# A gated linear-attention block and a PReLU network on one core: weight conversion reordered and split, gate products by scans, VectorE's order written out

## The chip, the cores and the metric

The kernel runs on one core of a Trainium2 chip. The metric is the device time of one execution in microseconds; three runs of the kernel before gave 783.32 us in the median (782.89 to 785.24). The core's engines are named as the profile names them: PE is TensorE (PEld its weight loads), DVE is VectorE, ACT is ScalarE, POOL is GpSimd, and SP is SyncE, which here only issues DMAs.

## What is computed

Two blocks follow each other. The first is an attention with a decaying state, for 4 batches of 8 heads, 768 positions and head dimension 48; the second is a network with one hidden layer of 2048 units on the 3072 rows (width 384) that the first one gives.

```python
f = 1.0 / (1.0 + np.exp(-f_logit))
for t in range(S):
    state = f[:, :, t, :, None] * state + np.einsum('bhd,bhe->bhde', k[:, :, t], v[:, :, t])
    y[:, :, t] = np.einsum('bhd,bhde->bhe', q[:, :, t], state)
x = y.transpose(0, 2, 1, 3).reshape(B * S, H * D)
h = x @ w_in                                            # 384 x 2048
g = np.maximum(h, 0.0) + alpha * np.minimum(h, 0.0)
out = g @ w_out                                         # 2048 x 384
```

All inputs are 32-bit floats but the two weight matrices, which arrive as 64-bit floats. The kernel turns them into 32-bit floats on the chip: each 64-bit value is read as two 32-bit words, and exponent, mantissa and sign are rebuilt with integer and float operations.

## The kernel before, in words

The work is cut into 12 chunks: 2 batches (U) by 128 positions (C), in the order of `steps`. The main loop runs over 13 steps; step n does the attention of chunk n and the network of chunk n-1, so that TensorE has network matmuls to do while VectorE works on the attention.

**Preparation of a chunk** (before the first `yield` of `attention`). The gate f goes through a sigmoid on ScalarE (L163). VectorE forms products of neighbouring gates: `kr` and `fq` within groups of four positions (L174 to L178), `qd`, the queries times one to three gates (L182, 3 operations), `us`, the queries times products of gates over further groups (L187 and six at L196), and `k4`, the keys times gates (L191). `pre` and `suf`, the running gate products from the left and from the right over the eight groups of a block of 32, are made on GpSimd by doubling (L203 to L212: a memset, a copy and 14 multiplications). Seven VectorE operations then make `q3`, `ks`, `kh` and `f64` from them (L222 to L232).

**Stages of a chunk** (five, with a `yield` behind each). For each of the two batches: TensorE makes `raw` (L246) and `qu` (L262), and VectorE copies the wanted parts into `ad` with predicated copies (L253, 4 of them; L267, 7 of them): these are stages 1 and 2. Stage 3: `off` (L280) and the transpose `pk` (L288), which ScalarE copies to `ksn` (L291). Stage 4: `pd` (L301) and the new states on VectorE (L311 to L315). Stage 5: ScalarE spreads `ad` and `off` into `A` (L323, L327), TensorE makes `py` (L336, L347), ScalarE copies it to `y` (L352), and ten DMAs issued by SP carry it into `xT` (L358), the network's input. `raw`, `qu`, `off`, `pk`, `pd` and `py` take turns in two PSUM buffers (tag `pair`).

**The network of a chunk.** In eight pieces of 256 hidden units: six matmuls to a PSUM bank `ph` (L371; the profile counts each as two), ScalarE makes `neg`, the part below zero (L376), and VectorE adds it back scaled, two operations to `g` (L379). Then for each batch 16 matmuls to `po` (L386), a copy on ScalarE (L389) and a DMA out. `ph` and `po` take turns in four PSUM banks.

**The weights** are converted by `load_weights` in 24 pieces of 512 columns, 12 for each matrix: a DMA issued by ScalarE (L129) and seven VectorE operations (L134 to L143). The pieces of `w_in` are called behind the stages of step 0 and those of `w_out` behind the stages of step 1, each matrix in the order in which it lies in memory: for `w_in` the whole first third of the input rows, then the second, then the third.

**The order of the work.** `tc.manual_schedule` takes TensorE's order as the program writes it: within a step two pieces of the network follow stage 1, two follow stage 2, then one, two and one, and all of `po` comes at the end of the step. All other engines run in the order that a scheduler finds. Each engine runs its instructions strictly one after another; an instruction that waits holds up those behind it, the DMA issues on SP's and ScalarE's queues too.

## Time and profile before

| what | value |
|---|---|
| median of the runs | 783.32 us |
| the profiled execution's own time | 781.1 us |
| its span, first to last instruction | 779.2 us |
| PE busy | 658.2 us (84%) |
| PEld busy | 485.5 us (62%) |
| DVE busy | 435.6 us (56%) |
| ACT busy | 159.1 us (20%) |
| POOL busy | 70.6 us (9%) |
| mean granted TensorE clock | 0.936 |

All rows of the trace are those of the profiled execution; 1.9 us of its time lie outside the span. In the views, a row of a group gives its line, engine and operation, what it writes and reads, its shapes and count, then after the bar the busy time in all and the mean of one in ns, and then the idle time of the engine just before these instructions with what ended it. In a timeline the first two numbers are the start and the length in us, and a bracket gives the idle time before.

### The profile page before, as it was taken

How to read it: one execution, taken by the hardware profiler on the slowest of the kernel's cores; microseconds unless marked ns; L12 is line 12 of the kernel's file. 1: busy time of each engine (PE TensorE's matmuls, PEld its weight loads, DVE VectorE, ACT ScalarE, POOL GpSimd, SP SyncE). 2: the span in 40 equal slices, each digit the busy share in tenths (PEclk: the TensorE clock that was granted, in tenths of full speed). 3: DMA queues.
4: the chain of work that ended last, by engine and by line, in shares of the span. 5: the costliest groups of instructions: out<-in, count | busy, mean ns of one | idle time of the engine just before them, and what ended most of it. 6: DMA issues, size and time to landing. Idle time of an engine off the chain costs nothing.

```text
span 779.2 us, 17567 instructions
## 1 busy us (share of the span) xinstructions
PE 658.2 (84%) x7712; PEld 485.5 (62%) x7712; DVE 435.6 (56%) x920; ACT 159.1 (20%) x289; POOL 70.6 (9%) x228
## 2 busy tenths in 40 slices
PE   0350186468999999899999999999999999999998
PEld 0350175124876777777867857768778678587684
DVE  5798997892861842933916808618439157052030
ACT  2030023000330411410411403204104114041110
POOL 8212002000020020020020100200200200000000
PEclk9995589557999999999999999999999999999999
DMA  4224432440220210211212202202101110000000
GB/s 177 83 84 122 159 105 76 135 145 26 69 67 21 84 42 22 83 41 28 80 48 66 56 24 70 65 22 83 41 23 55 51 40 8 24 13 22 21 0 21
DMA packets 31468, 46.79 MB, mean 60 GB/s; under 512 B 3744, under 2 KB 19104, under 8 KB 31392
## 3 DMA queue, kind: packets, MB, share of 16 engines
q1 hardware_dynamic: 27648, 33.04, 14.2%
q10 hardware_dynamic: 3744, 12.63, 5.1%
q8 instruction: 61, 1.00, 0.5%
q14 instruction: 15, 0.12, 0.1%
HBM read 36.22 MB, written 4.72 MB: 53 GB/s over the span
## 4 chain that ended last, share of the span: by engine, by line
PE 67%; DVE 21%; DMA 5%; POOL 3%; ACT 1%; issue 1%; SPq 1%; ACTq 0%; DVEq 0%; POOLq 0%
PE po L386 31%; PE ph L371 24%; PE py L336 3%; DVE qd L182 3%; PE py L347 3%; DVE g L379 2%; DVE ad L267 2%; PE raw L246 2%; DMA qd<-in_qT 2%; DVE ad L253 2%; PE pd L301 2%; PE pk L288 2%; PE qu L262 1%; DMA w_in_raw<-in_w_in 1%; DMA w_out_raw<-in_w_out 1%; DVE k L191 1%
## 5 line engine op out<-in xcount | busy, mean ns | idle before, releaser
L371 PE MATMUL ph<-xT,w_in_sb 128*128 128x256 f32 x1152 | 269.2, 390 | 37.5 <-DVE w_in_sb L143 37.5
L386 PE MATMUL po<-w_out_sb,g 128*128 128x384 f32 x768 | 264.5, 504 | 29.3 <-DVE w_out_sb L143 29.3
L371 PEld LDWEIGHTS ph<-xT,w_in_sb 128*128 128x128 f32 x1152 | 218.4, 194 | 73.0 <-DVE w_in_sb L143 39.2
L386 PEld LDWEIGHTS po<-w_out_sb,g 128*128 128x128 f32 x768 | 149.0, 196 | 140.5 <-DVE w_out_sb L143 32.9
L253 DVE COPY_PREDICATED ad<-mraw,raw 128x256 f32<-128x256 int32 x96 | 42.7, 444 | 174.6 <-PE raw L246 172.4
L379 DVE SCALAR_TENSOR_TENSOR g<-neg,om,ph 128x256 f32<-128x256 f32 x192 | 84.3, 475 | 72.5 <-ACT neg L376 72.2
L376 ACT ACTIVATE neg<-ph 128x512 f32<-128x512 f32 x96 | 57.3, 597 | 201.6 <-PE ph L371 131.8
L389 ACT COPY o<-po 128x384 f32<-128x384 f32 x24 | 11.5, 478 | 278.5 <-PE po L386 278.5
L267 DVE COPY_PREDICATED ad<-mquad,qu 128x224 f32<-128x224 int32 (+6 forms) x168 | 49.7, 296 | 5.2 <-DVE ad L253 0.5
L246 PE MATMUL raw<-qd,k 48*32 48x128 f32 x1536 | 29.4, 286 | 19.4 <-DVE qd L182 19.4
L196 DVE TENSOR_TENSOR us<-us,fq 128x768 f32<-128x768 f32 (+2 forms) x72 | 44.3, 615 | 0.0
L203 POOL MEMSET suf<- 128x256 f32 x12 | 3.7, 311 | 418.4 <-DVE ks L225 418.4
L246 PEld LDWEIGHTS raw<-qd,k 48*32 48x32 f32 x1536 | 22.8, 110 | 28.5 <-POOL pre L212 19.4
L262 PE MATMUL qu<-us,k 48*32 48x116 f32 x1536 | 27.3, 273 | 12.4 <-DVE us L196 6.9
L323 ACT COPY A<-ad 32x512 f32<-32x512 f32 x48 | 29.6, 617 | 20.1 <-DVE ad L267 19.7
L262 PEld LDWEIGHTS qu<-us,k 48*32 48x32 f32 x1536 | 22.5, 109 | 13.7 <-DVE us L196 7.3
L232 DVE TENSOR_TENSOR f<-pre 128x16 f32<-128x16 f32 x12 | 2.2, 184 | 47.8 <-POOL pre L212 47.7
L210 POOL TENSOR_TENSOR suf<-suf,pre 128x32 f32<-128x32 f32 (+2 forms) x84 | 28.8, 368 | 1.8
L182 DVE TENSOR_TENSOR qd<-qd,f 128x768 f32<-128x768 f32 (+2 forms) x36 | 27.5, 764 | 1.9 <-DMA qd<-in_qT 1.8
L336 PE MATMUL py<-A,v 128*64 128x128 f32 x384 | 24.9, 285 | 2.5 <-DVE us L196 2.5
L288 PE MATMUL pk<-ident,ks 128*128 128x128 f32 x96 | 13.9, 291 | 14.5 <-DVE ad L267 11.7
L336 PEld LDWEIGHTS py<-A,v 128*64 128x64 f32 x384 | 22.0, 143 | 6.3 <-issue 6.3
(60 smaller groups left out, 429.8 us busy)
## 6 DMA issues: line engine op xcount, KB each, us to landing
f<-in_fT SPq DMA_DIRECT2D x12, 512.0 KB, 3.7
k<-in_kT SPq DMA_DIRECT2D x12, 512.0 KB, 5.5
qd<-in_qT SPq DMA_DIRECT2D x12, 512.0 KB, 4.0
w_in_raw<-in_w_in ACTq DMA_DIRECT2D x12, 512.0 KB, 3.5
w_out_raw<-in_w_out ACTq DMA_DIRECT2D x12, 512.0 KB, 3.5
v<-in_v SPq DMA_DIRECT2D x12, 384.0 KB, 3.3
out<-o SPq DMA_DIRECT2D x24, 192.0 KB, 1.9
xT<-y SPq DMA_DIRECT2D x72, 48.0 KB, 2.0
```

The costliest lines, as they stand in the source:

```text
L182: nc.vector.tensor_tensor(quads(qdv[d])[:, :, d:4], quads(qdv[d - 1])[:, :, d:4], f[:, :, 1:5 - d], ALU.mult)
L196: nc.vector.tensor_tensor(us[:, :, UO[m]:UO[m] + 4 * n].rearrange("p g (i r) -> p g i r", r=4), us[:, :, skip:skip + 4 * n].rearrange("p g ...
L246: nc.tensor.matmul(raw[DB * j:DB * (j + 1), par, hp * C:(hp + 1) * C], lhsT=k[r_, g:g + DB], rhs=qd[r_, 0:4 * W].rearrange("p (d x) -> p d ...
L253: nc.vector.copy_predicated(adu, mraw[:, d].rearrange("p i r -> p (i r)").bitcast(I32).unsqueeze(1).broadcast_to((128, H, DB)), rv[:, :, d])
L262: nc.tensor.matmul(qu[DB * j:DB * (j + 1), par, hp * UW:(hp + 1) * UW], lhsT=k4[r_, g * DB:(g + 1) * DB], rhs=us[r_, g], start=True, stop= ...
L267: nc.vector.copy_predicated(ad[:, u, :, :, 4 * m:DB], mquad[:, lo:lo + n].bitcast(I32).unsqueeze(1).unsqueeze(1).broadcast_to((128, 2, HP, ...
L323: nc.scalar.copy(A[s_, :, :, s_], ad[s_].rearrange("p u r h t -> p u (r h) t"))
L336: nc.tensor.matmul(py[64 * par:64 * par + 64, u, hp * C:(hp + 1) * C], lhsT=vt[:, u, hd * D:hd * D + 64], rhs=A[:, u, par * HP + hp], star ...
L371: nc.tensor.matmul(ph[:, j * T:(j + 1) * T], lhsT=w_in_sb[:, kt, (f + j) * 128:(f + j + 1) * 128], rhs=xT[:, kt], start=(kt == 0), stop=(k ...
L376: nc.scalar.activation(neg, phv, AF.Relu, scale=-1.0)
L379: nc.vector.scalar_tensor_tensor(g[:, j], neg[:, j], om[:, f + j:f + j + 1], phv[:, j], ALU.mult, ALU.add)
L386: nc.tensor.matmul(po[:, 0:DM], lhsT=gs[f // 2][:, f % 2, u * C:(u + 1) * C], rhs=w_out_sb[:, f], start=(f == 0), stop=(f == NF - 1))
```

## The change

1. **Conversion.** Per piece five VectorE operations instead of seven, and one on ScalarE: the exponent field is masked out on VectorE, shifted to its new base on ScalarE (an activation with a scale and a bias, clamped at zero), and sign and mantissa are joined by shifts and ORs on whole integers, where the old code built a float mantissa by parts. Each piece has its own buffers (four for the raw words). The DMAs of the pieces are issued by SP instead of ScalarE.
2. **Order of the pieces.** `w_in` is converted in groups of three pieces, one of each third of the input rows, so that three pieces serve the first two `ph` of a network. `load_weights` is a generator whose pieces are called one by one between other work.
3. **Gate products.** `pre` and `suf` come from two scans on VectorE per chunk, of 289 elements each, in place of GpSimd's 16 operations. The factors lie in `fs` with a zero between blocks, and `ones` restarts the product there. GpSimd keeps one small memset per chunk.
4. **Order.** VectorE's order is now written out too. The preparation of a chunk is a sequence of seven pieces. A step is a string of calls: S is a stage of the chunk, P a piece of its own preparation, Q a piece of the next chunk's, n a piece of the network of the chunk before, w and v a piece of `w_in` and `w_out`. Steps 0 to 3 have strings of their own.
5. **Network.** The two `po` of a chunk are filled side by side, four f at a time in pieces of their own (12 pieces per network in all).
6. **Smaller edits.** Queries are loaded into a tile of their own and copied to `qd` by ScalarE (1024 elements); five of the ten `xT` DMAs are issued by ScalarE; `om` is made by ScalarE instead of VectorE; GpSimd's memsets of `qd` and `kr` at the start cover only what needs it; several tiles have one buffer less (`v`, `y`, `q3`, `ks`, `kh`: one; `neg`: two; `g`: eight).

```diff
-    nc.vector.tensor_scalar(om, om, -1.0, 1.0, ALU.mult, ALU.add)
+    nc.scalar.activation(om, om, AF.Identity, bias=1.0, scale=-1.0)
...
-        for n in range(0, flat.shape[1], WP):
-            raw = work.tile([128, WP, 2], I32, tag="y", name=f"{name}_raw{n}")
-            nc.scalar.dma_start(out=raw.rearrange("p n two -> p (n two)"),
-                                in_=src[:, n:n + WP].bitcast(I32))
+        ks = NK if dst is w_in_sb else 1
+        per = flat.shape[1] // ks
+        for n in [k * per + j for j in range(0, per, WP) for k in range(ks)]:
+            raw = work.tile([128, WP, 2], I32, tag="raw", name=f"{name}_raw{n}", bufs=4)
+            nc.sync.dma_start(out=raw.rearrange("p n two -> p (n two)"),
+                              in_=src[:, n:n + WP].bitcast(I32))
             lo, hi = raw[:, :, 0], raw[:, :, 1]
-            mi = work.tile([128, WP], I32, tag="neg", name=f"{name}_mi{n}", bufs=3)
-            nc.vector.tensor_scalar(mi, hi, 0xFFFFF, 0x100000, ALU.bitwise_and, ALU.bitwise_or)
-            m = mi.bitcast(F32)
-            nc.vector.scalar_tensor_tensor(m, lo.bitcast(U32), 2.0 ** -32, mi, ALU.mult, ALU.add)
-            e = work.tile([128, WP], I32, tag="neg", name=f"{name}_e{n}", bufs=3)
-            nc.vector.tensor_scalar(e, hi, 20, 0x7FF, ALU.logical_shift_right, ALU.bitwise_and)
-            nc.vector.tensor_scalar(e, e, 1023.0 - 127.0, 0.0, ALU.subtract, ALU.max)
-            nc.vector.tensor_scalar(e, e, 255.0, 2.0 ** 23, ALU.min, ALU.mult)
+            e = work.tile([128, WP], I32, tag="e", name=f"{name}_e{n}")
+            nc.vector.tensor_scalar(e, hi, 0x7FF00000, None, ALU.bitwise_and)
+            nc.scalar.activation(e, e, AF.Relu, bias=bias, scale=8.0)
+            m = work.tile([128, WP], U32, tag="m", name=f"{name}_m{n}")
+            nc.vector.tensor_scalar(m, hi.bitcast(U32), 11, 0x80000000, ALU.logical_shift_left, ALU.bitwise_or)
+            nc.vector.scalar_tensor_tensor(m, lo.bitcast(U32), 21, m, ALU.logical_shift_right, ALU.bitwise_or)
             nc.vector.scalar_tensor_tensor(e, hi, -0x80000000, e, ALU.bitwise_and, ALU.bitwise_or)
-            nc.vector.scalar_tensor_tensor(flat[:, n:n + WP], m, 2.0 ** -20, e.bitcast(F32), ALU.mult, ALU.mult)
+            nc.vector.scalar_tensor_tensor(flat[:, n:n + WP], m, 2.0 ** -31, e.bitcast(F32), ALU.mult, ALU.mult)
+            yield
...
-        h = 1
-        while h < NB:
-            for n in range(0, NB, 2 * h):
-                lo, up = slice(n, n + h), slice(n + h, n + 2 * h)
-                nc.gpsimd.tensor_tensor(suf[:, :, lo], suf[:, :, lo],
-                                        pin[:, :, n + 2 * h - 1:n + 2 * h].broadcast_to((128, G, h)), ALU.mult)
-                nc.gpsimd.tensor_tensor(pin[:, :, up], pin[:, :, up],
-                                        pin[:, :, n + h - 1:n + h].broadcast_to((128, G, h)), ALU.mult)
-            h *= 2
+        ps = work.tile([128, NS], F32, tag="ps", name=f"ps_{i}", bufs=1)
+        nc.vector.tensor_tensor_scan(ps, fs, ones, 0.0, ALU.mult, ALU.add)
+        ss = work.tile([128, NS], F32, tag="ss", name=f"ss_{i}", bufs=1)
+        nc.vector.tensor_tensor_scan(ss[:, ::-1], fs[:, ::-1], ones[:, ::-1], 0.0, ALU.mult, ALU.add)
...
-                nc.sync.dma_start(
+                (nc.sync if hd % 2 else nc.scalar).dma_start(
...
+    first = (
+        "P7 S w S w S w S w S w2",
+        "n w n w n w n w n w n w n2 P7 S v S v S v S v2 S v n2 v3 n v3 n",
...
+    usual = "S n Q n S n Q n S Q n S Q n Q n S Q2 n5"
```

What this moves shows at three places. First VectorE at the start of the first network, where `g_0_0` is made: the last conversion of `w_in` in the kernel before,

```order
L134 TENSOR_SCALAR w_in_mi_578<-w_in_raw_576 128x512
L143 SCALAR_TENSOR_TENSOR w_in_sb<-w_in_mi_567,w_in_e_570 128x512
L136 SCALAR_TENSOR_TENSOR w_in_mi_578<-w_in_raw_576,w_in_mi_578 128x512
L139 TENSOR_SCALAR w_in_e_581<-w_in_raw_576 128x512
L140 TENSOR_SCALAR w_in_e_581<-w_in_e_581 128x512
L379 SCALAR_TENSOR_TENSOR g_0_0_729<-neg_0_0_727,om,ph_0_0_720 128x256
```

and the same place now, where the seventh of twelve pieces stands behind the first `g`:

```order
L394 SCALAR_TENSOR_TENSOR g_0_0_520<-neg_0_0_518,om,ph_0_0_511 128x256 x2
L148 TENSOR_SCALAR w_in_e_525<-w_in_raw_523 128x512
L152 TENSOR_SCALAR w_in_m_528<-w_in_raw_523 128x512
L153 SCALAR_TENSOR_TENSOR w_in_m_528<-w_in_raw_523,w_in_m_528 128x512
L154 SCALAR_TENSOR_TENSOR w_in_e_525<-w_in_raw_523,w_in_e_525 128x512
L155 SCALAR_TENSOR_TENSOR w_in_sb<-w_in_m_528,w_in_e_525 128x512
L394 SCALAR_TENSOR_TENSOR g_0_0_542<-neg_0_0_540,om,ph_0_0_533 128x256 x2
L148 TENSOR_SCALAR w_in_e_547<-w_in_raw_545 128x512
```

Before, the first `g` stands in the last of the twelve pieces; now six pieces come ahead of it and one piece behind each of the first six `g`.

Second, VectorE in the middle of a usual step: the copies out of the second `qu` of a chunk into `ad`, before, with work for the next chunk (`k`, `qd`) between them,

```order
L379 SCALAR_TENSOR_TENSOR g_1_1_2356<-neg_1_1_2354,om,ph_1_1_2347 128x256 x2
L253 COPY_PREDICATED ad<-mraw,raw_0_2_2359 128x256 x4
L267 COPY_PREDICATED ad<-mquad,qu_0_2_2396 128x8x28
L191 TENSOR_TENSOR k_1_2_2682<-k_2_2667,kr 128x1024
L267 COPY_PREDICATED ad<-mquad,qu_0_2_2396 128x8x24
L182 TENSOR_TENSOR qd<-qd,f_2_2663 128x256x3
L267 COPY_PREDICATED ad<-mquad,qu_0_2_2396 128x8x20
L182 TENSOR_TENSOR qd<-qd,f_2_2663 128x256x2
```

and now:

```order
L394 SCALAR_TENSOR_TENSOR g_1_2_3243<-neg_1_2_3241,om,ph_1_2_3234 128x256 x2
L182 TENSOR_TENSOR kr<-f_3_3246 128x256
L183 TENSOR_TENSOR kr<-f_3_3246,kr 128x256
L186 TENSOR_TENSOR fs<-f_3_3246,kr 128x32x8
L394 SCALAR_TENSOR_TENSOR g_1_2_3266<-neg_1_2_3264,om,ph_1_2_3257 128x256 x2
L266 COPY_PREDICATED ad<-mraw,raw_0_3_3269 128x256 x4
L280 COPY_PREDICATED ad<-mquad,qu_0_3_3306 128x8x28
L280 COPY_PREDICATED ad<-mquad,qu_0_3_3306 128x8x24
L280 COPY_PREDICATED ad<-mquad,qu_0_3_3306 128x8x20
```

The three gate products of the next chunk now come ahead of these copies, and nothing comes between the copies; `qd` follows behind the next `g`.

Third, ScalarE at the end of the first chunk's attention, where `y` is copied. Before, DMA issues for weights follow the copy,

```order
L163 ACTIVATE f_1_1663<-f_1_1663 128x1024
L352 COPY y_0_442<-py_0_409 128x512 x2
L129 DMA w_in_raw_455<-in_w_in 128x1024
L129 DMA w_in_raw_466<-in_w_in 128x1024
L129 DMA w_in_raw_477<-in_w_in 128x1024
```

and now five issues for `xT` (two alike in the fifth row), and behind them the exponents of the fifth and sixth piece of `w_in`:

```order
L365 COPY y_0_477<-py_0_444 128x512 x2
L372 DMA xT_0_480<-y_0_477 48x2x128
L372 DMA xT_0_480<-y_0_477 32x2x128
L372 DMA xT_0_480<-y_0_477 16x2x128
L372 DMA xT_0_480<-y_0_477 48x2x128 x2
L149 ACTIVATE w_in_e_493<-w_in_e_493,bias 128x512
L149 ACTIVATE w_in_e_503<-w_in_e_503,bias 128x512
L391 ACTIVATE neg_0_0_518<-ph_0_0_511 128x512
```

The exponents of two conversions now queue behind DMA issues on ScalarE, and VectorE's conversion of those pieces waits for them.

126 lines of the change are left out of this document (68 added, 58 removed), and 2 rows, old and new, of the table first.

## The prediction

> **What bounds the kernel now.** I read the page's slices first, then the windows by stage, then who waited for whom, then the timelines of PE and DVE. The slices, 19.5 us each, show two kernels in one:
>
> ```profile
> PE   0350186468999999899999999999999999999998
> DVE  5798997892861842933916808618439157052030
> PEclk9995589557999999999999999999999999999999
> ```
>
> In the first ten slices DVE is full, PE is mostly idle, and PE's clock drops to half. Behind them PE is full. The windows put numbers on it; a row gives the window, its length, then the busy time of PE, PEld, DVE, ACT and POOL, and the granted clock:
>
> ```profile
> 0.00:194.80 194.80, 88.82 (x1072) 58.88 (x1072) 152.10 (x304) 26.06 (x43) 32.47 (x93) 0.75 0.35 111
> 194.80:359.50 164.70, 159.51 (x1945) 119.66 (x1944) 88.14 (x189) 39.33 (x72) 14.41 (x51) 0.99 0.18 52
> 359.50:681.90 322.40, 315.89 (x3897) 237.16 (x3902) 173.29 (x372) 76.08 (x141) 23.70 (x84) 1.00 0.16 47
> 681.90:734.50 52.60, 52.60 (x650) 39.82 (x650) 15.07 (x39) 11.38 (x22) 0.00 (x0) 1.00 0.06 17
> 734.50:779.20 44.70, 41.33 (x160) 30.02 (x158) 6.98 (x16) 6.21 (x11) 0.00 (x0) 1.00 0.04 14
> 413.20:466.90 53.70, 52.65 (x657) 39.55 (x661) 29.31 (x63) 13.13 (x24) 4.80 (x17) 1.00 0.19 53
> ```
>
> 194.8 us go by before step 2 starts: the start. Steps 2 to 4 take 164.7 us, steps 5 to 10 322.4 us (53.7 each, of which PE is busy 52.65, one of them in the last row), step 11 52.6 us, the last network 44.7 us. So a usual step has 1.05 us to give, and the start has some 130 us in which PE is not at work at full clock. The waits name the two places (us in total, times, longest):
>
> ```profile
> PE ph L371 <- DVE w_in_sb L143: 37.5, 3, 17.2
> PE po L386 <- DVE w_out_sb L143: 29.3, 12, 9.0
> PE pk L288 <- DVE ad L267: 11.7, 9, 2.4
> DVE f L232 <- POOL pre L212: 47.7, 10, 4.8
> ```
>
> PE's large waits are for converted weights. `pk` waits for the predicated copies nine times. The 47.7 us that DVE waits for POOL's products are cover: DVE has over 20 us of idle time in a usual step.
>
> **The change, part by part.** First the prices. A conversion now:
>
> ```profile
> 80.27 0.43 DVE L134 TENSOR_SCALAR w_in_mi<-w_in_raw 128x512 int32<-128x512 int32 x1
> 101.67 0.42 DVE L134 TENSOR_SCALAR w_in_mi<-w_in_raw 128x512 int32<-128x512 int32 x1
> L142 DVE SCALAR_TENSOR_TENSOR w_in_e<-w_in_raw,w_in_e 128x512 int32<-128x512 int32 x12 | 8.3, 690 | 0.3
> L376 ACT ACTIVATE neg<-ph 128x512 f32<-128x512 f32 x96 | 57.3, 597 | 201.6 <-PE ph L371 131.8 <-DVE w_in_sb L143 48.3 <-issue 19.3
> ```
>
> The two L134 are six pieces apart: 3.57 us a piece, where four short operations (0.43) and three long ones (0.69) add up to 3.79, so starts overlap by 6%. The new piece has two short and three long: 2.93 by durations, 2.8 as I take it; 24 of them save 24 x 0.77 = 18 us of DVE. The exponent goes over ScalarE: 0.6 us by `neg`, the same size; on integers it is not in the trace, and I bound it by half and double that. It runs beside the two DVE operations between (0.43 + 0.69 = 1.1 us), so it is free if ScalarE takes it at once, and costs what ScalarE is late if not. The Trainium skill ("ScalarE: Activation LUTs", What ACT_TABLE_LOAD costs) gives an activation with a bias from memory 280 ns plus 0.833 ns per element, here 0.71 us; by it the sum would be up to 24 x 0.1 = 2.4 us longer. No row here has such a bias.
>
> The preparation of a chunk on DVE:
>
> ```profile
> L174 DVE TENSOR_TENSOR kr<-f 128x256 f32<-128x256 f32 x12 | 7.6, 633 | 1.9 <-POOL kr L116 1.9
> L182 DVE TENSOR_TENSOR qd<-qd,f 128x768 f32<-128x768 f32 (+2 forms) x36 | 27.5, 764 | 1.9 <-DMA qd<-in_qT 1.8
> L187 DVE TENSOR_TENSOR us<-qd,f 128x1024 f32<-128x1024 f32 x12 | 24.1, 2011 | 0.0
> L191 DVE TENSOR_TENSOR k<-k,kr 128x1024 f32<-128x1024 f32 x12 | 14.6, 1216 | 0.0
> L196 DVE TENSOR_TENSOR us<-us,fq 128x768 f32<-128x768 f32 (+2 forms) x72 | 44.3, 615 | 0.0
> L222 DVE TENSOR_TENSOR q<-us,pre 128x512 f32<-128x512 f32 x24 | 16.3, 680 | 0.0
> ```
>
> Per chunk: three like L174 (1.9), `qd` 27.5/12 = 2.3, `us` 2.0 and 44.3/12 = 3.7, `k4` 1.2, and six like L222 with a tiny one (4.1): 15.2 us. Two scans come on top. No row shows one: 289 elements by L174 would be 0.7 us, by L222 0.4; as each element waits for the one before it could be double the slower, 1.4, and a gain is excluded because DVE had no such work. I take 0.5 each, near L222, whose operands lie side by side as the scan's do: 16.2 us per chunk. The Trainium skill ("DVE: opcode table, instruction layouts, handler registers and perf-mode slots", Datapath and trigger behaviour) has this scan run at half throughput; by it two preparations in the start would be 4 x 0.4 = 1.6 us longer; no row of this trace shows it. In usual steps DVE's idle time hides either. GpSimd's products cost nothing where they were, and going they gain nothing but the 3 us that `kh` waited once in the start.
>
> The copies of one batch into `ad`, and a pair of `g`:
>
> ```profile
> 360.73 1.89 DVE L253 COPY_PREDICATED ad<-mraw,raw 128x256 f32<-128x256 int32 x4 [18.62 <-PE raw L246]
> 362.72 2.29 DVE L267 COPY_PREDICATED ad<-mquad,qu 128x224 f32<-128x224 int32 x7
> 364.99 0.87 DVE L379 SCALAR_TENSOR_TENSOR g<-neg,om,ph 128x256 f32<-128x256 f32 x2
> ```
>
> 4.3 us for the eleven copies, 0.87 for the `g`. The start and the way out of the first chunk:
>
> ```profile
> 1.67 1.28 ACT L163 ACT_TABLE_LOAD   x1 [1.67 <-PEq L472]
> 4.52 1.06 ACT L163 ACTIVATE f<-f 128x1024 f32<-128x1024 f32 x1 [1.57 <-DMA f<-in_fT]
> 9.34 0.64 DVE L174 TENSOR_TENSOR kr<-f 128x256 f32<-128x256 f32 x1 [1.85 <-POOL kr L116]
> 41.50 1.97 PE L288 MATMUL pk<-ident,ks 128*128 128x128 f32 x8 [1.44 <-ACT A L327]
> 49.10 3.26 PE L336 MATMUL py<-A,v 128*64 128x128 f32 x32 [2.51 <-DVE us L196]
> 52.29 1.10 PE L347 MATMUL py<-q,state 48*48 48x64 f32 x32
> 53.93 0.59 ACT L352 COPY y<-py 128x512 f32<-128x512 f32 x1
> 54.54 6.94 SPq L358 DMA_DIRECT2D xT<-y  x10
> 62.96 1.22 PE L371 MATMUL ph<-xT,w_in_sb 128*128 128x256 f32 x2 [7.30 <-DVE w_in_sb L143]
> ```
>
> *Up to the first `ph`.* `om` on ScalarE brings a second table load of 1.28 us ahead of the sigmoid, which ends near 7.4 instead of 5.6; but DVE waited for GpSimd's memset of `kr` until 9.34, and that wait goes. DVE starts at 7.4, ends the preparation at 23.6, copies of batch 0 at 27.9, a weight piece at 30.7, copies of batch 1 at 35.0. Now PE has `pk` to `py`, which took 11.9 us (41.50 to 53.39) with a 2.5 us wait in it: 9.4, done at 44.4. On DVE weight pieces and the states lie beside it. `y` takes 1.1 us; the ten `xT` issues take 0.69 us each on one queue, so five on each of two 3.5 us; landing took 1.5 us (61.48 to 62.96). First `ph` at 50.5, with its weights there.
>
> *The first network and w_in.* The first `ph` runs at half clock. These two rows are the same twelve matmuls, at half clock in part and warm:
>
> ```profile
> 113.38 4.37 PE L371 MATMUL ph<-xT,w_in_sb 128*128 128x256 f32 x12
> 212.09 2.76 PE L371 MATMUL ph<-xT,w_in_sb 128*128 128x256 f32 x12
> 392.45 20.80 PE L386 MATMUL po<-w_out_sb,g 128*128 128x384 f32 x64
> ```
>
> With 4.8 us for it, `neg` and `g`, DVE stands at 56.9. From here DVE is the pace: six pieces and five `g`, 6 x 2.8 + 5 x 0.87 = 21.2, to 78.1. The last two `ph`, partly cold, 6.8, then `neg` and `g` 1.5: 86.4. PE's other six `ph` lie under the pieces.
>
> *Second chunk and w_out.* Preparation 16.2 to 102.6; twice 4.3 of copies, six pieces (16.8) and three state operations of at most 0.68: 27.4, to 130. Two exponents queue behind five `xT` issues on ScalarE (3.5 us); I add 3: 133. Six more pieces: 149.8. `po` of the first 12 f lies beside them; the last four f are 16 of the 64 rows of `po`, 5.2 us. Step 2 starts at 155, not 194.8: 39.8 us gained.
>
> *Given back in steps 2 and 3.* Their chunks are prepared inside the step. In step 2 the second `raw` waits for copies that stand behind eight `g` and the preparation (2.6 for the first `ph`, 0.6 for `neg`, 8 x 0.87, 16.2 and 1.9 make 28.3; PE, after eight `ph` of 2.6, about 2 for `raw` and `qu` and 5.2 for a piece of `po`, is there at 28), `qu` then 1.2, `pd` 1.1 for `ksn`, and the next network 2 for `xT`, since only one piece of `po` (5.2 us) lies behind `py`: 52.6 + 4.8 = 57.4. Step 3 has 2.4 of such waits: 55. With step 4 at 52.7 the three make 165.1, against 164.7.
>
> *Usual steps.* PE's order is as before. `pk` no longer waits: by these rows and the step's start at 359.5 PE reaches it 15.3 us into the step,
>
> ```profile
> 374.08 0.76 PE L280 MATMUL off<-q,kh 48*32 48x32 f32 x64
> ```
>
> and DVE, with `kr` and two pairs of `g` ahead, ends the copies at about 13.3 (5.5 + 0.87 + 1.9 + 0.87 + 4.3). The copy of q to `qd` on ScalarE (1.06 by the sigmoid's row) and the issues fit into 40 us of its idle time. Steps 5 to 10: 316.2, against 322.4. Step 11 stays 52.6. At the end two copies of `po` stand behind the last matmul instead of one: 44.7 + 0.3.
>
> **Sum:** 155 + 165.1 + 316.2 + 52.6 + 45.0 = 733.9, against a span of 779.2: 45.3 less. The profiled execution took 781.1, so 735.8; its median is 783.3, 2.2 above it, and I forecast 783.3 - 45.3 = 738.
>
> **The rivals.**
>
> *A. ScalarE holds up the conversion.* If each exponent meets a `neg`, a copy or issues ahead of it, 0.6 to 1.1 us per piece are exposed: 24 times that less the 3 I have, 11 to 23 us: 749 to 761. For it: the third order shows just that. Against: ScalarE is busy 26 of 194.8 us. 0.13.
>
> *B. The usual step keeps a wait of 1 us,* at `pd`, since ScalarE now copies `off` and part of `ad` ahead of `ksn`. Eight steps, 8 us: 746. For it: `pk` to `pd` leaves ScalarE only one `ph`, 2.6 us. 0.14.
>
> *C. The start is shorter.* Preparations overlap by the same 6% as conversions (2 us), PE is warm earlier (4), steps 2 and 3 hide their waits (4): 728. 0.10.
>
> *D. Slower than before.* DVE can no longer step over an instruction that waits. In a usual step `kr` of the next chunk stands ahead of the copies; if its sigmoid is late, `g`, `raw`, `qu` and `pk` all are. The slack is 15.3 - 13.3 = 2 us; to lose 45.3 us in eight steps it must be 2 + 5.7 = 7.7 us late in each. At 10 us late: 738 + 8 x 8 = 802. Against it: f is loaded a step ahead. 0.05, of which 0.01 near no change.
>
> *E. The change doesn't do what it says:* the interleaving brings no overlap and only the cheaper conversion is left: 783 - 18 = 765. For it: DVE's 152 us of work in the start, less 18, are still 134. Against: PE waits 66.8 us for weights there, which now come in its order. 0.03.
>
> **How the numbers follow.** My case has 0.55 and its own range of 731 to 747 (the scans' and ScalarE's bounds above, PE's clock below). The range 722 to 758 takes in C, B and most of A. A measurement of this kernel can tell about 0.3% (its three runs lie 0.3% apart). Faster by more: 0.55 + 0.13 + 0.14 + 0.10 + 0.03 = 0.95; within: 0.01; slower: 0.04.
>
> **What would show it.** Right: first `ph` near 50, the first `raw` of step 2's chunk behind PE's eighth `ph` of that step, that step starting near 155; usual steps of 52.7 with no wait of `pk`; conversions of 2.8 us; scans near 0.5. DVE's wait for L149 over 0.5 us per piece would be A; a wait of `pd` for `ksn` B; DVE idle before `kr` for the sigmoid D. Wrong: a first `ph` past 60, step 2 past 175, or usual steps over 54.

## The result and the profile after

The changed kernel takes 734.5 us in the median of four runs (733.24 to 738.78), the kernel before 783.71 us on the same chip: a ratio of 0.938, with a 95% interval of 0.934 to 0.942. The forecast was 738. The profiled execution took 733.96 us with a span of 732.2; all rows of the changed kernel are from it.

The slices of the changed kernel, 18.3 us each, stand first:

```profile
PE   1368436889998999999999999999999999999997
DVE  5969698869639588548458368279088186250020
PEclk9989855999999999999999999999999999999999
```

PE is full from the tenth slice on (its start at 165 us) instead of the eleventh (195 us), and the clock is at half in two slices instead of four. DVE in the first eight slices goes up and down between half and all of its time. The windows of the changed kernel, cut where its stages begin (length, then busy time of PE, PEld, DVE, ACT and POOL, granted clock):

```profile
0.00:152.80 152.80, 84.39 (x1072) 62.30 (x1073) 121.06 (x233) 45.56 (x70) 7.75 (x33) 0.84 0.43 138
152.80:319.00 166.20, 160.82 (x1952) 119.47 (x1953) 111.79 (x218) 43.62 (x78) 0.37 (x3) 0.99 0.18 55
319.00:635.00 316.00, 316.00 (x3932) 237.60 (x3937) 191.10 (x388) 80.93 (x148) 0.74 (x6) 1.00 0.16 47
635.00:687.40 52.40, 52.40 (x627) 39.57 (x612) 15.60 (x40) 11.20 (x22) 0.00 (x0) 1.00 0.06 17
687.40:732.20 44.80, 41.00 (x159) 29.74 (x157) 6.98 (x16) 5.88 (x11) 0.00 (x0) 1.00 0.05 18
```

The start went from 194.8 to 152.8 us. DVE's busy time in it fell by 152.1 - 121.1 = 31 us and its idle time from 42.7 to 31.7. Steps 5 to 10 fell from 322.4 to 315.4 us, from their own first matmul at 318.96 to that of step 11 at 634.40 (the third row is cut 0.6 us behind it), and PE is busy in all of that time. Steps 2 to 4 gave 1.4 us back. POOL is busy for 8.9 us in all, where it was 70.6. The waits of the changed kernel (us in total, times, longest) in place of those of before:

```profile
PE raw L259 <- DVE qd L193: 18.9, 2, 13.1
PE ph L386 <- DVE w_in_sb L155: 8.0, 3, 2.8
DVE w_in_e L154 <- ACT w_in_e L149: 5.3, 3, 4.1
PE po L402 <- DVE w_out_sb L155: 4.7, 4, 1.2
DVE w_out_e L154 <- ACT w_out_e L149: 2.8, 2, 1.9
```

PE's waits for weights are down from 66.8 us to 12.7, and DVE's new waits for ScalarE's exponents are 8.1 us in all. How the start runs now, on PE:

```profile
51.14 1.19 PE L386 MATMUL ph<-xT,w_in_sb 128*128 128x256 f32 x2 [3.96 <-DMA xT<-y]
52.55 13.41 PE L386 MATMUL ph<-xT,w_in_sb 128*128 128x256 f32 x50 [0.22 <-DMA xT<-y]
68.77 5.01 PE L386 MATMUL ph<-xT,w_in_sb 128*128 128x256 f32 x22 [2.81 <-DVE w_in_sb L155]
76.16 0.70 PE L386 MATMUL ph<-xT,w_in_sb 128*128 128x256 f32 x2 [2.38 <-DVE w_in_sb L155]
79.67 6.85 PE L386 MATMUL ph<-xT,w_in_sb 128*128 128x256 f32 x20 [2.81 <-DVE w_in_sb L155]
92.32 1.96 PE L259 MATMUL raw<-qd,k 48*32 48x128 f32 x64 [5.79 <-DVE qd L193]
...
150.14 2.85 PE L402 MATMUL po<-w_out_sb,g 128*128 128x384 f32 x8 [1.17 <-DVE w_out_sb L155]
152.83 3.40 PE L386 MATMUL ph<-xT,w_in_sb 128*128 128x256 f32 x15
```

The first `ph` comes at 51.1 us instead of 63.0 and now waits for `xT`, no longer for a weight. The first network's `ph` end at 86.5. Step 2 begins with the last row. In a usual step `pk` follows `off` without a wait:

```profile
386.08 0.76 PE L293 MATMUL off<-q,kh 48*32 48x32 f32 x64
386.77 1.09 PE L301 MATMUL pk<-ident,ks 128*128 128x128 f32 x8
387.70 2.76 PE L386 MATMUL ph<-xT,w_in_sb 128*128 128x256 f32 x12
```

### The profile page after: what moved, and what is told of

The parts are those of the page before. It is cut to its first block, busy times and chain, and to the rows that moved or that the text cites. A ratio compares the mean times of both kernels' runs of the same rounds, so it can differ in the third digit from the quotient of the medians.

```text
span 732.2 us, 17405 instructions
## 1 busy us (share of the span) xinstructions
PE 654.6 (89%) x7712; PEld 488.7 (67%) x7712; DVE 446.5 (61%) x895; ACT 187.2 (26%) x327; POOL 8.9 (1%) x42
## 3 DMA queue, kind: packets, MB, share of 16 engines
q1 hardware_dynamic: 25536, 43.26, 18.7%
## 4 chain that ended last, share of the span: by engine, by line
PE 78%; DVE 17%; ACT 2%; issue 1%; DMA 1%; ACTq 1%; DVEq 0%
PE ph L386 31%; PE po L402 31%; PE py L349 4%; PE py L360 3%; PE raw L259 2%; PE qu L275 2%; DVE us L210 2%; PE pk L301 2%; DVE ad L280 2%; PE pd L314 2%; DVE g L394 2%; DVE ad L266 1%; PE off L293 1%; DVE qd L193 1%; DVE w_out_sb L155 1%
## 5 line engine op out<-in xcount | busy, mean ns | idle before, releaser
L402 PE MATMUL po<-w_out_sb,g 128*128 128x384 f32 x768 | 252.6, 488 | 4.7 <-DVE w_out_sb L155 4.7
L402 PEld LDWEIGHTS po<-w_out_sb,g 128*128 128x128 f32 x768 | 144.7, 190 | 105.1 <-DVE w_out_sb L155 8.5
L210 DVE TENSOR_TENSOR us<-us,fs 128x768 f32<-128x768 f32 (+2 forms) x72 | 44.9, 624 | 2.1
L275 PE MATMUL qu<-us,k 48*32 48x116 f32 x1536 | 29.3, 288 | 13.0 <-DVE us L210 9.9
L349 PE MATMUL py<-A,v 128*64 128x128 f32 x384 | 27.0, 300 | 2.4 <-issue 1.2
L349 PEld LDWEIGHTS py<-A,v 128*64 128x64 f32 x384 | 23.9, 152 | 6.4 <-issue 5.1
L199 DVE TENSOR_TENSOR us<-qd,f 128x1024 f32<-128x1024 f32 x12 | 24.1, 2009 | 0.1
L360 PE MATMUL py<-q,state 48*48 48x64 f32 x704 | 22.9, 221 | 0.0
L360 PEld LDWEIGHTS py<-q,state 48*48 48x48 f32 x704 | 21.1, 123 | 2.4 <-issue 2.4
L180 ACT ACTIVATE f<-f 128x1024 f32<-128x1024 f32 x12 | 12.7, 1057 | 36.1 <-DMA f<-in_fT 36.1
```

Of the source, the lines that this page charges most:

```text
L210: nc.vector.tensor_tensor(us[:, :, UO[m]:UO[m] + 4 * n].rearrange("p g (i r) -> p g i r", r=4), us[:, :, skip:skip + 4 * n].rearrange("p g ...
L275: nc.tensor.matmul(qu[DB * j:DB * (j + 1), par, hp * UW:(hp + 1) * UW], lhsT=k4[r_, g * DB:(g + 1) * DB], rhs=us[r_, g], start=True, stop= ...
L349: nc.tensor.matmul(py[64 * par:64 * par + 64, u, hp * C:(hp + 1) * C], lhsT=vt[:, u, hd * D:hd * D + 64], rhs=A[:, u, par * HP + hp], star ...
L360: nc.tensor.matmul(py[64 * par:64 * par + D, u, o:o + CH], lhsT=states[cc][r_, u * HP + hp], rhs=qs[r_, u, hp, cc, 0:CH], start=False, sto ...
L402: nc.tensor.matmul(po[u][:, 0:DM], lhsT=gs[f // 2][:, f % 2, u * C:(u + 1) * C], rhs=w_out_sb[:, f], start=(f == 0), stop=(f == NF - 1))
```

## The experiments

The theory going in was the prediction's: the cheaper conversion and the smaller amount of VectorE work ahead of step 2 make the start shorter, VectorE's written order takes the `pk` wait out of the usual steps, and ScalarE's exponents and the scans cost little. The first seven runs take its parts away one at a time, the last five follow a finding of the fifth. Unless a diff says otherwise, the kernel edited is the changed one, and "step 2 begins" means its first matmul on PE, 152.8 us in the changed kernel, and 194.8 in the kernel before.

**The old conversion in the new order.**

```diff
-            nc.vector.tensor_scalar(e, hi, 0x7FF00000, None, ALU.bitwise_and)
-            nc.scalar.activation(e, e, AF.Relu, bias=bias, scale=8.0)
...
+            nc.vector.tensor_scalar(e, hi, 20, 0x7FF, ALU.logical_shift_right, ALU.bitwise_and)
+            nc.vector.tensor_scalar(e, e, 1023.0 - 127.0, 0.0, ALU.subtract, ALU.max)
+            nc.vector.tensor_scalar(e, e, 255.0, 2.0 ** 23, ALU.min, ALU.mult)
...
```

> The changed kernel, but with the seven VectorE operations of the old conversion in each piece and none on ScalarE; order, buffers and DMAs stay. Theory (VectorE's work paces the start): some 20 of 24 pieces lie on the path, each longer by about 0.75 us, less the 4 us in which VectorE waits for ScalarE's exponents on the path: 11 us longer, about 745 us. Rival (the overlap that the order brings is the gain, not the cheaper conversion): at most 3 us longer, about 737 us.

Measured: 748.23 us, ratio 0.955 (0.952 to 0.958), 13.7 us above the changed kernel. PE's waits for weights are longer again, 13.8 us where the changed kernel has 8.0:

```profile
PE ph L388 <- DVE w_in_sb L157: 13.8, 4, 3.9
```

Step 2 begins at 166.7, 13.9 later, and nothing is made up afterwards. VectorE is busy for 142.95 us ahead of it instead of 121.06, so 21.9 more; its waits for exponents, 8.1 us, are gone; 21.9 - 8.1 = 13.8. So what a piece costs VectorE beyond those waits is paid in full in the start.

**All of w_in first, in memory order.** The pieces are converted in the order of before, and all twelve ahead of the first `g`.

```diff
-        ks = NK if dst is w_in_sb else 1
+        ks = 1
...
-        "P7 S w S w S w S w S w2",
-        "n w n w n w n w n w n w n2 P7 S v S v S v S v2 S v n2 v3 n v3 n",
+        "P7 S w S w S w S w S w8",
+        "n8 P7 S v S v S v S v2 S v n2 v3 n v3 n",
```

> The changed kernel, but w_in is converted in the order of memory and all twelve pieces stand ahead of the first g. Theory (VectorE's work paces the start): VectorE has the same work, only TensorE's last ph move back, about four of them (10 us) against two now, and g with them: 2 to 5 us longer, 737 to 740 us. Rival (the order of need is the gain): all eight ph, 20.7 us, now lie behind the pieces and the first chunk: about 15 us longer, 750 us.

Measured: 735.69 us, ratio 0.937 (0.934 to 0.940): no different from the changed kernel, and just under the theory's range. PE waits 1.6 us and then once for long, and runs 92 of the 96 `ph` records in one go:

```profile
65.08 23.08 PE L386 MATMUL ph<-xT,w_in_sb 128*128 128x256 f32 x92 [9.69 <-DVE w_in_sb L155]
93.93 1.96 PE L259 MATMUL raw<-qd,k 48*32 48x128 f32 x64 [5.78 <-DVE qd L193]
```

Chunk 1's `raw`, behind all of it, starts 1.6 us later than in the changed kernel. The order of need lets PE do most of the `ph` sooner, but VectorE, which sets the end of this stretch, has the same work either way.

**The products on GpSimd again,** as in the kernel before, without scans.

```diff
-        nc.vector.tensor_tensor_scan(ps, fs, ones, 0.0, ALU.mult, ALU.add)
...
+                nc.gpsimd.tensor_tensor(suf[:, :, lo], suf[:, :, lo],
+                                        pin[:, :, n + 2 * h - 1:n + 2 * h].broadcast_to((128, G, h)), ALU.mult)
...
```

> The changed kernel, but pre and suf are made on GpSimd as before and the two scans go. Theory (VectorE paces the start, GpSimd's products are hidden beside qd, us and k4): 1.5 us less VectorE work in each of two preparations in the start and about 1 us in steps 2 and 3: 3 to 5 us shorter, about 730 us. Rival (GpSimd's chain of about 6 us ends late, or slows VectorE while both work): 0 to 5 us longer, 735 to 740 us.

Measured: 731.40 us, ratio 0.9327 (0.9305 to 0.9349), a little under the changed kernel. Step 2 begins at 153.85, 1.0 us later; from there to the end it takes 728.9 - 153.85 = 575.1 us instead of 732.2 - 152.83 = 579.4. The gain lies in steps 2 and 3, where the preparation on VectorE is on the path. In step 3 the second `raw` of the changed kernel waits 1.41 us for copies and its `qu` 1.26, and the granted clock over that `qu` and the 24 `ph` behind it is 0.79; with the products on GpSimd that `raw` does not wait, and the clock stays at 1.00, which is 1.6 us of the gain. The scans, part of a kernel that is faster as a whole, cost about 3 us, of which this part hangs on the clock.

**Chunk 2 prepared in the start,** ahead of the second half of `w_out`; nothing else moves.

```diff
-        "n w n w n w n w n w n w n2 P7 S v S v S v S v2 S v n2 v3 n v3 n",
-        "n P n P n P n P n P n P n P n S n S n S2 n S Q3 n",
+        "n w n w n w n w n w n w n2 P7 S v S v S v S v2 S v Q7 n2 v3 n v3 n",
+        "n7 n S n S n S2 n S Q3 n",
```

> The changed kernel, but the preparation of chunk 2 (seven pieces, 16.7 us of VectorE with the scans) is called in step 1, ahead of the second half of w_out, as the kernel before had it in its start. Theory (VectorE's work paces the start): step 2 begins 15 to 17 us later, and gives back 2 to 4 us there: about 747 us. Rival (the start is paced by TensorE and transfers, or this work hides under po): within 3 us of the changed kernel, 732 to 738 us.

Measured: 751.49 us, ratio 0.958 (0.954 to 0.961), 17 us above the changed kernel and 4 above what the theory gave, as the later steps gave nothing back. `po` waits for `w_out`:

```profile
153.74 4.58 PE L402 MATMUL po<-w_out_sb,g 128*128 128x384 f32 x8 [15.95 <-DVE w_out_sb L155]
```

Step 2 begins at 170.1, 17.2 later, about one preparation; from there to the end it takes 579.4 us, as in the changed kernel. Where the preparation stands is worth more than the conversion.

**VectorE's order left to the scheduler,** TensorE's written as before.

```diff
-    with tc.manual_schedule(engines={mybir.EngineType.PE, mybir.EngineType.DVE}):
+    with tc.manual_schedule(engines={mybir.EngineType.PE}):
```

> The changed kernel, but VectorE's order is left to the scheduler again (TensorE's stays written out). Theory (the written order removes the wait of pk and keeps each piece where it is needed): usual steps get back about 1 us each, 8 us, and the start a few us either way: 740 to 746 us. Rival (the scheduler finds as good an order from the same calls): 733 to 736 us.

Measured: 743.29 us, ratio 0.947 (0.944 to 0.951), 8.8 us above the changed kernel, inside the theory's range. The total alone would have passed for a confirmation. The timeline of PE shows two large effects that nearly cancel:

```profile
51.72 22.68 PE L386 MATMUL ph<-xT,w_in_sb 128*128 128x256 f32 x94 [0.26 <-DMA xT<-y]
...
130.32 20.88 PE L386 MATMUL ph<-xT,w_in_sb 128*128 128x256 f32 x96
...
324.15 1.06 PE L301 MATMUL pk<-ident,ks 128*128 128x128 f32 x8 [3.02 <-DVE ad L280]
325.05 2.76 PE L386 MATMUL ph<-xT,w_in_sb 128*128 128x256 f32 x12
...
379.78 1.53 PE L301 MATMUL pk<-ident,ks 128*128 128x128 f32 x8 [3.02 <-DVE ad L280]
381.10 4.01 PE L386 MATMUL ph<-xT,w_in_sb 128*128 128x256 f32 x12
```

The start is 22.5 us *shorter*: step 2 begins at 130.3, and `ph` never waits for a weight. A usual step is longer: `pk` waits 3.02 us. In the first of the two shown that is all. In the second PE loses its clock (0.68 granted over the last two rows) and takes 1.53 instead of 1.09 for `pk` and 4.01 instead of 2.76 for the twelve `ph` behind it; 3.02 + 0.44 + 1.25 = 4.7. Steps 5 to 10 take 55.6 or 57.3 us, three of them each, where those of the changed kernel take 52.6. VectorE in the second, where the copies that `pk` waits for are spread out by work for the next chunk:

```profile
373.39 0.40 DVE L280 COPY_PREDICATED ad<-mquad,qu 128x224 f32<-128x224 int32 x1
373.69 0.64 DVE L193 TENSOR_TENSOR qd<-qd,f 128x256 f32<-128x256 f32 x1
374.23 0.38 DVE L280 COPY_PREDICATED ad<-mquad,qu 128x192 f32<-128x192 int32 x1
374.49 2.01 DVE L199 TENSOR_TENSOR us<-qd,f 128x1024 f32<-128x1024 f32 x1
376.40 0.33 DVE L280 COPY_PREDICATED ad<-mquad,qu 128x160 f32<-128x160 int32 x1
```

So the written order earns its gain in the steps behind the start and costs some 22 us in the start. Before the change, the free order lost 1.05 us in a usual step; in the changed kernel it loses 3.0 to 4.7. Which of the edits makes the scheduler's order worse there, no run shows.

**All xT issues on SP.**

```diff
-                (nc.sync if hd % 2 else nc.scalar).dma_start(
+                nc.sync.dma_start(
```

> The changed kernel, but all ten xT transfers of a chunk are issued by SyncE as before. Theory: the first ph and the ph of step 3, which wait for xT, come 2 to 3 us later each; the exponents of two pieces in step 1 no longer stand behind issues, 3 us sooner: 735 to 738 us. Rival (issues on ScalarE's queue cost more than they bring): 731 to 733 us.

Measured: 735.82 us, ratio 0.938 (0.935 to 0.941), the same as the changed kernel. PE waits 9.4 us for `xT` instead of 4.2, and the exponents that queued behind ScalarE's issues come sooner; the two trade evenly. The rival, a gain from freeing ScalarE, is out.

**The new conversion alone in the kernel before.**

> The kernel before with the new conversion alone (five VectorE operations and the exponent on ScalarE); order, buffers and the issues by ScalarE stay. Theory (VectorE's work paces the start): 24 x 0.77 = 18 us shorter, less some waits for exponents: 766 to 772 us. Rival (cheaper conversion alone brings little, since transfers on ScalarE's queue and exponents now wait for each other): 776 to 783 us.

Measured: 766.55 us, ratio 0.977 (0.974 to 0.981), 18.7 us less than the kernel before on the same chip (785.24). In the profiled executions step 2 begins at 179.4, 15.4 earlier, and the span of 766.6 is 12.6 shorter; but this execution (768.42) was the longest of its four, and the one of the kernel before (781.1) was shorter than its median. With the 13.8 us that the first experiment shows in the span of the changed kernel, the conversion is worth some 13 to 19 us; whether it is worth the same in both orders, the runs do not settle.

**A free start, written later steps.** VectorE's order is the scheduler's in steps 0 and 1, and the program's from step 2 on.

```diff
+    for written, ns in (({PE}, range(0, 2)), ({PE, DVE}, range(2, len(steps) + 1))):
+        with tc.manual_schedule(engines=written):
+            for n in ns:
...
```

> VectorE's order is left to the scheduler in steps 0 and 1 and written by the program from step 2 on (TensorE's written throughout). Theory, that the free order wins in the start and the written one in the later steps, and that the two are independent: step 2 begins at about 130 us, as in the free order (130.3), instead of 152.8; steps 2 to 4 take 166, steps 5 to 10 315.4 and the rest 97.8, as in the changed kernel; span about 710, time 711 to 717. Rival, that the free start is short only because it hands work on (pieces of chunk 2's preparation and w_out's last pieces): step 2 gives most of it back and the time is 728 to 735.

Measured: 710.72 us, ratio 0.906 (0.903 to 0.909), just under the theory's range. Step 2 begins at 128.1 and the rest takes 707.5 - 128.1 = 579.4 us, to the tenth what the changed kernel takes: nothing is handed on. The window of its start holds the same counts of instructions as the changed kernel's:

```profile
0.00:128.00 128.00, 76.97 (x1072) 59.48 (x1073) 110.52 (x233) 45.03 (x70) 7.78 (x33) 0.87 0.49 164
```

It is the same work in another order. Of the 24.8 us, 10.5 are busy time of DVE (121.06 to 110.52 for 233 instructions each, where time in which two overlap counts once), and 14.3 idle time. The durations of the single instructions add up to 130.1 us there and 129.3 here, so 9.8 of the 10.5 is overlap. Rows of VectorE show where it comes from. In the changed kernel an instruction that uses the result of the one ahead follows it with a small gap:

```profile
29.30 0.42 DVE L152 TENSOR_SCALAR w_in_m<-w_in_raw 128x512 uint32<-128x512 uint32 x1
29.76 0.69 DVE L153 SCALAR_TENSOR_TENSOR w_in_m<-w_in_raw,w_in_m 128x512 uint32<-128x512 uint32 x1
```

In the kernel whose order is free throughout they alternate with those of other pieces:

```profile
31.19 0.68 DVE L154 SCALAR_TENSOR_TENSOR w_in_e<-w_in_raw,w_in_e 128x512 int32<-128x512 int32 x1
31.79 0.69 DVE L153 SCALAR_TENSOR_TENSOR w_in_m<-w_in_raw,w_in_m 128x512 uint32<-128x512 uint32 x1
32.40 0.42 DVE L148 TENSOR_SCALAR w_in_e<-w_in_raw 128x512 int32<-128x512 int32 x1
```

Above, the first instruction ends at 29.72 and the next starts at 29.76, 0.04 later. Below, the first ends at 31.87 and the next has started at 31.79, 0.08 earlier. In the start of the changed kernel 115 instructions follow with such a gap, of 0.15 us at most, 4.4 us in all; in this kernel 6 do, 0.3 us in all. So the order of neighbours accounts for 9.8 us of overlap and for 4.2 of the idle time, some 14 us. Of the other idle time, 9.0 us are longer waits: VectorE's waits for `neg`, 8.0 us in the changed kernel, are gone, those for exponents are 2.6 less, and those for transfers of weights 1.7 more. The last 1.1 us are no matter of the order: VectorE's first instruction on the gates, which waits for the sigmoid, starts at 8.59 there and at 7.50 here, and anywhere from 7.3 to 8.8 in the kernels edited from the changed one, with VectorE's order written or free. It follows the landing of `om`, for which ScalarE waits ahead of the sigmoid (until 5.97 and 4.88 us).

**The same with GpSimd's products.**

> As the kernel with a free start, and the gate products on GpSimd as before the change, without the two scans. Theory: 3 us less than the kernel with the free start, as they were worth 3.1 us to the changed kernel, so 708 to 714, the gain in steps 2 to 4 again. Rival: the free start is bound by VectorE's work and waits for GpSimd's products in the start, so that the time is the same as that kernel's or up to 3 us more.

Measured: 710.74 us, ratio 0.906 (0.903 to 0.908), no different from the one with scans. The theory's 3 us are not there, and the rival holds: step 2 begins at 133.85, 5.8 later, and the rest takes 575.2 us, 4.3 less. VectorE waits 6.5 us for GpSimd's products in this start. Of the 5.8, 1.2 are the later sigmoid (VectorE's first instruction on the gates at 8.70 instead of 7.50).

**Chunk 1's preparation among the last gates,** all in written order.

```diff
-        "n w n w n w n w n w n w n2 P7 S v S v S v S v2 S v n2 v3 n v3 n",
+        "n w n w n w n w n w n w P3 n P2 n P2 S v S v S v S v2 S v n2 v3 n v3 n",
```

> VectorE's order written throughout; only chunk 1's preparation stands among network 0's last gates (three pieces of it after the last piece of w_in, two after the seventh gate, two after the eighth) instead of behind them all. Theory: VectorE's idle 4.56 and 2.20 us behind ph at 80 to 88 us are filled, chunk 1's second quad products and all behind them come 6 to 7 us sooner: 727 to 729. Rival, that the start is bound by TensorE's waits for w_in (2.81, 2.38, 2.81), which stay: 733 to 735.

Measured: 728.05 us, ratio 0.929 (0.925 to 0.932), 6.5 less than the changed kernel. PE's waits for weights stay, but `raw` no longer waits for the preparation:

```profile
79.95 6.84 PE L386 MATMUL ph<-xT,w_in_sb 128*128 128x256 f32 x20 [2.81 <-DVE w_in_sb L155]
86.72 1.16 PE L259 MATMUL raw<-qd,k 48*32 48x128 f32 x64
```

Step 2 begins at 146.2, 6.6 us earlier. It was VectorE's idle time behind the gates, not PE's wait for weights, that cost.

**And the exponent one piece ahead.**

```diff
+            begun.append((n, lo, hi, e))
+            if len(begun) == 1:
+                continue
+            finish(*begun[-2])
...
```

Here `finish` holds the last four VectorE instructions of a piece.

> As the kernel with chunk 1's preparation early, and each weight piece's first VectorE instruction and its exponent on ScalarE stand one piece ahead of the other four, so that VectorE's fourth no longer waits for ScalarE. Theory, that the waits for the exponent (5.3 us with w_in, 2.8 with w_out) are on the path once VectorE bounds the start: 5 to 8 us less than the kernel with the preparation early alone, 719 to 724. Rival, that they lie under the wait for xT and for chunk 1's pieces: 726 to 729, the same as that kernel. Both stay above the kernel with the free start (711 to 717), because the free order also lets independent instructions follow each other, each starting 0.09 us before the end of the one ahead.

Measured: 724.19 us, ratio 0.923 (0.920 to 0.926): between the theory's range and the rival's, and the two intervals just overlap. DVE's waits for exponents fall to 2.2 and 0.9 us, from 5.5 and 2.9 with the preparation early alone, but step 2 begins only 1.6 us sooner (144.57), so most of these waits lie under other ones: its waits for `neg` are 3.9 us, where they were 1.1. The other 1.5 us of the span are PE's clock in step 3. In the changed kernel, and so with the preparation early alone, `raw` and `qu` wait 1.41 and 1.26 us there and the clock falls (0.79 granted over these two rows):

```profile
230.78 1.61 PE L275 MATMUL qu<-us,k 48*32 48x116 f32 x64 [1.26 <-DVE ad L280]
232.32 6.50 PE L386 MATMUL ph<-xT,w_in_sb 128*128 128x256 f32 x24
```

In this kernel they wait as long, and it stays at 1.00:

```profile
222.65 1.09 PE L284 MATMUL qu<-us,k 48*32 48x116 f32 x64 [1.26 <-DVE ad L289]
223.66 5.45 PE L395 MATMUL ph<-xT,w_in_sb 128*128 128x256 f32 x24
```

**Scans in the start, GpSimd later.** The kernel with the free start, with scans for chunks 0 and 1 alone.

```diff
+        if steps.index((bp, c)) < 2:
             nc.vector.tensor_tensor_scan(ps, fs, ones, 0.0, ALU.mult, ALU.add)
             nc.vector.tensor_tensor_scan(ss[:, ::-1], fs[:, ::-1], ones[:, ::-1], 0.0, ALU.mult, ALU.add)
+        else:
...
+            nc.gpsimd.tensor_copy(pin, fq)
```

> Free order in steps 0 and 1, scans for chunks 0 and 1 alone, the products of all later chunks on GpSimd. Theory, that the scans gain in the start and cost in steps 2 and 3: the start of the kernel with the free start (128.1 us to step 2's first matmul) and the later steps of its GpSimd variant (709.0 - 133.9 = 575.1 us): span 703.2, time 705 to 707. Rival, that the two differences (5.8 us of start, 4.3 us later) are of the scheduler's order in each whole kernel and not of the place of the products: 709 to 711, like both.

Measured: 706.82 us, ratio 0.9025 (0.899 to 0.906). Step 2 begins at 129.8, 1.7 later than with scans throughout (the first 1.0 of it at the sigmoid), and the rest takes 575.2 us. The place of the products decides, as expected; its median is the lowest of all kernels here, 28 us under the changed one. Its interval still overlaps those of the two other kernels with a free start.

## Why the prediction was right, and where it was not

By its own steps, with the rows of the changed kernel:

| step | forecast | measured |
|---|---|---|
| chunk 0's preparation begins | 7.4 | 8.6 |
| chunk 0's `py` done | 44.4 | 47.2 |
| first `ph` | 50.5 | 51.1 |
| network 0's last `ph` and `g` done | 86.4 | 88.1 |
| chunk 1's preparation | 16.2 | 16.1 (88.04 to 104.12) |
| `w_out`'s last piece done | 149.8 | 150.1 |
| step 2 begins | 155 | 152.8 |
| steps 2 to 4 | 165.1 | 166.1 |
| steps 5 to 10 | 316.2 | 315.4 |
| step 11 and the last network | 97.6 | 97.8 |
| span | 733.9 | 732.2 |

The working was right in its mechanism: VectorE sets the pace of the start, its work there was counted piece by piece, and PE's order sets the rest. The forecast of 738 is 3.5 us above the median. Of that, 1.7 us are the span, and 1.8 the step from span to median: the median lay 4.1 us above the span of the profiled execution before and 2.3 after.

**Luck.** Some rows agree by errors that cancel. The sigmoid ends at 8.56 us where I had 7.4, since `om`, which ScalarE now makes ahead of it, waits for its transfer until 5.97. Chunk 0's `py` is done 2.8 us late. The first `ph` is only 0.6 late because `xT` takes 4.0 us from there where I had 6.1: PE starts before the last of the ten transfers is issued (issues until 52.06), and the 1.5 us for the landing I had read from a row in which PE waited for weights, not for `xT`. In a preparation the scans are 0.5 us longer than my 1.0 for both, and the other instructions 14.6 where I had added up 15.2, as many overlap a little.

**Scans.** I took 0.5 us, by the row whose operands lie side by side. They took 0.75 and 0.73. The groups of the changed kernel, with different shapes apart:

```profile
L210 DVE TENSOR_TENSOR us<-us,fs 128x768 f32<-128x768 f32 x12 | 11.4, 953 | 0.0
L210 DVE TENSOR_TENSOR us<-us,fs 128x128 f32<-128x128 f32 x12 | 3.5, 292 | 0.4
L219 DVE TENSOR_TENSOR_SCAN ps<-fs,ones 128x289 f32<-128x289 f32 x12 | 9.0, 753 | 0.0
L221 DVE TENSOR_TENSOR_SCAN ss<-fs,ones 128x289 f32<-128x289 f32 x12 | 8.8, 732 | 0.0
L149 ACT ACTIVATE w_in_e<-w_in_e,bias 128x512 int32<-128x512 int32 x12 | 8.6, 720 | 24.8 <-DVE w_in_e L148 21.3 <-DMA xT<-y 3.5
```

The two rows of L210 give 661 ns for 640 elements, so 1.03 ns each, and 0.16 us beside them; at twice that per element a scan of 289 would take 0.16 + 0.60 = 0.76. So the rule that I had set beside my value, by the Trainium skill ("DVE: opcode table, instruction layouts, handler registers and perf-mode slots", Datapath and trigger behaviour) half throughput for this scan, agrees with the rows, and my estimate by it (0.4 more per scan) was on the high side. A preparation still came out at 16.1 us. That "GpSimd's products cost nothing where they were" holds in the written order, where having them back costs 1.0 us in the start (some 2.3 if the sigmoid, 1.3 sooner in that execution, is set aside) and gains 4.3 behind it; in a free start, where VectorE is denser, they cost 5.8 (4.6 in the same way).

**The exponent** took 0.72 us where I took 0.6 by `neg`. The estimate of 0.71 by what the Trainium skill gives for an activation with a bias from memory ("ScalarE: Activation LUTs", What ACT_TABLE_LOAD costs) agrees with the row. The 2.4 us that hung on it do not show: where ScalarE takes it at once, the 1.1 us of VectorE work beside it still cover it.

**Rival A** (ScalarE holds up the conversion) had its five waits, 8.1 us in all, where I had 3, but four of them are under 2 us, and the longest, 4.1 us at the `xT` issues, lies under PE's wait for `xT`: VectorE, done with that piece and the next, still waits 1.26 us for the first `neg`. Issuing `xT` elsewhere gained nothing, and taking the exponent one piece ahead 1.6 us at step 2. **Rival B** did not come: no wait of `pd` in a usual step. **Rival D** did not either: `kr` waits for its sigmoid only at the very start (4.03 us). **Rival C**, a shorter start, gave 2.2 us, hardly for its reasons: the last stretch of `po` behind the last weights is 8 records, 2.85 us, where I had 16 and 5.2.

**Rival E** was the instructive one. It said that interleaving the pieces brings no overlap. The order of need in itself indeed brought nothing (second experiment), and still the start fell by 42 us. The conversion gives 13.9 of them, chunk 2's preparation that has left the start 17.2 (the two experiments that undo them): together 31.1, and VectorE ends its last weight piece 31.0 us sooner. The remaining 10.9 lie behind that piece. In the kernel before, one `po` was filled ahead of the other, and the whole second one came behind the last weights:

```profile
181.17 13.71 PE L386 MATMUL po<-w_out_sb,g 128*128 128x384 f32 x36 [1.67 <-DVE w_out_sb L143]
```

Now both fill side by side, and 8 records, 2.85 us, are left. That this is the fifth part of the change is read from the rows; no run undoes it alone. I had all three in the sum, without naming the preparation as the largest.

**What no step of mine considered** is that VectorE's written order could lose time. I counted what it does to `pk` in the usual steps (1.05 us in the kernel before; in the changed one 3.02 if VectorE's order is left free, none if written), and costed it in the start at nothing, though "DVE can no longer step over an instruction that waits" stood under rival D. The free start is 24.8 us shorter, and some 14 of them are neighbours that depend on each other: 9.8 of overlap and 4.2 of small gaps. 6.6 us are the preparation of chunk 1, which the program puts behind all gates, and 1.6 the exponents. 1.1 are the sigmoid's start, which is not the order's, and 0.8 shorter instructions; what is left, under 1 us, was not taken apart. With both of the last two written orders VectorE's longer waits are 11.7 us, as in the free start (11.2), so it is the neighbours that still part them.

## What to carry over

A total that comes out as forecast does not show that every part pays: leave one part of the change out and read both stages, since here a gain of about 33 us behind the start and a loss of 22 in it stood behind a difference of 9. An engine's written order pays where a due time has to be kept against other work (the copies that `pk` waits for), and loses where the engine is simply full and a scheduler can fill its waits; the two can be had in one program. Where a written order has to fill an engine, set instructions side by side that do not use each other's results: of the 24.8 us some 14 were such neighbours, though no run here wrote an order that way. Work in the start is paid, but for what fits into waits, while one engine bounds it: ask of every instruction there whether a later stage, with idle time on that engine, could take it.

## What the runs showed of the hardware

- VectorE starts an instruction 0.08 us before the end of the one ahead if it does not need its result, and 0.04 us after it if it does (rows above). Over the 233 instructions of the start the order made 9.8 us of overlap and 4.2 us of gaps. The Trainium skill ("VectorE: DVE Perf Modes", The DRAIN you can't avoid) has eight copies take the same time with a semaphore after each and with one after the last alone, though it lets a next instruction that is not held start earlier; here neighbours that depend on each other are slower, and for this kernel the measurement decides.
- Waits of PE of the same length lose the clock in one step and not in the next. With VectorE's order free, `pk` waits 3.0 us in each of steps 5 to 10: in three of them the clock falls (in one, twelve `ph` take 4.01 us against 2.76), in three it stays at 1.00 over `pk` and these `ph`. Waits of 1.41 and 1.26 us close together lost it in the changed kernel and did not with the exponents ahead. With 1.05 us per usual step, as in the kernel before, it stayed at 1.00. The Trainium skill ("TensorE: Matmul & The Clock Gate", Part 1) has the clock judged in windows of about 3.4 us that run on freely; that the place of a wait decides and not its length alone fits this, but no run moved a wait to test it.
- A small activation of another kind ahead of the sigmoid brought a second table load of 1.28 us: two loads at 1.74 and 6.20 us, where the kernel before had one. It also put the sigmoid behind the transfer of `om`: it starts at 7.50 us, where it started at 4.52 in the kernel before. VectorE waits 4.03 us for it; what `om` behind the sigmoid would gain, no run shows.

```profile
1.74 1.28 ACT L93 ACT_TABLE_LOAD   x1 [1.74 <-issue]
5.97 0.21 ACT L93 ACTIVATE om<-om 128x16 f32<-128x16 f32 x1 [2.95 <-DMA om<-in_alpha]
6.20 1.28 ACT L180 ACT_TABLE_LOAD   x1
```
